# A fused retention and gated-MLP block on one core: w_out requested sooner, fewer filler matmuls, and the residual of batch 4 turned by DMA transposes

## The chip, the core and the metric

The kernel runs on one core of a Trainium2 chip. The core has five engines that run side by side: TensorE (PE, with its weight loads shown as PEld), VectorE (DVE), ScalarE (ACT), GpSimd (POOL) and SyncE (SP), which here only issues DMAs. Sixteen DMA engines serve all the queues. The metric is the device time of one execution in microseconds (us). Three runs of the kernel before gave 213.83, 214.52 and 214.94 us; their median is 214.52 us.

## The reference

Retention first (8 batches, 8 heads, 576 positions, head size 64), then a gMLP block over the heads put side by side (512 wide), with the retention's output `x` as the residual:

```
scores = q @ k.T / sqrt(64);  ret = scores * gamma_h ** (i - j) for i >= j, else 0
x = (ret @ v), heads side by side: [8, 576, 512]
h = gelu_tanh(x @ w_in);  u, v = halves of h (512 each)
v_n = (v - mean(v)) / sqrt(var(v) + 1e-6) * g_ln
v_s = w_sg @ v_n (over the 576 positions) + b_sg
out = x + (u * v_s) @ w_out
```

All inputs and the output are float32. The kernel multiplies in bfloat16 and adds up in float32.

## The kernel before, in words

The work is cut into 18 steps, `j = 0..17`. Steps 0 and 9 take the first 64 positions of four batches at once; each other step takes 256 positions of one batch, so that steps 10 and 11 are the two halves of batch 4, and 12 to 17 those of batches 5, 6 and 7. Output rows come in tiles of 128: pair `p` of batches has nine of them, `m = 0..8`; tile 4 (`MID`) holds the first 64 positions of both batches.

One step goes through these stages. q, k and v arrive by DMA from SP. POOL scales q and k to bfloat16 (`qb`, `kb`) and casts v (`vb`), ACT and DVE doing some of them at the start. q and k are transposed: q by DMA transposes on SP from step 5 on (`turn`, L288), k on PE (`T`, L271), except for the last steps, where k too is turned by DMA. Then `quarters` (L451) makes on PE the scores `sc` of the next step, its state products `zp` and the outputs `ot` of this one; `intra` (L469) copies `ot` to `xT`, the retention's output, *transposed* (features on partitions). `V` and `U` multiply `xT` by the two halves of w_in. When a batch has both halves, `release` queues its units: `W` (the product over positions with w_sg, L600, and the product with u on DVE, L602) and `O` (the product with w_out, L622). The loop at L804 takes units from that list by the numbers in `slots`. The order on each engine is written out by hand: an engine runs its instructions in the order in which the program lists them, and SP and POOL issue DMAs in that order too.

The residual of an `O` unit is added in one of two ways. For batches 0 to 4, `xT` is turned back on PE: four matmuls of 128x128 with `xT` as weights and the identity as data (L626) add it to the product in PSUM, and ACT copies the tile to `ob` (L628). For batches 5 to 7 a DMA transpose on SP (`turn_x`, L297, issued at L304) has put the residual into `xn`, with rows on partitions; PE then does only the four matmuls of L622, and DVE adds `xn` while it empties PSUM (L630). The first tiles of the pairs (`m == MID`) use the first way, but for the last pair. A DMA of SP then stores the tile (L635).

Three other places bear on the change. At the start, `spin(16)` (L672) runs 48 matmuls on zeros of 171, 171 and 170 columns while the first data arrive. The weights w_out are fetched by a DMA that POOL issues, since it casts to bfloat16 (`load_w(SB)`, L187). And step 3's state product ends in `cast_zb` on POOL (L391), which waits for a DVE addition (L390).

Of the kernel before, what the change touches and what calls it, by code (L numbers as in the profile page):

```python
# [12 lines left out]
BF = mybir.dt.bfloat16  # L13
# [6 lines left out]
def kernel(  # L20
# [193 lines left out]
    idle = psD.tile([128, 512], F32, name="idle", tag="d")  # L214
    SPIN = 171, 171, 170

    def spin(n):
        for _ in range(n):
            for c in SPIN:
                nc.tensor.matmul(idle[:, :c], fill[:, :128], fill[:, :c], start=True, stop=True)  # L220


# [15 lines left out]
    def xT(p, m):  # L238

        b = 2 * p + (m > MID)  # L240
        if m == MID:
            if (p, m) not in xTs:
                xTs[p, m] = xup.tile([128, KK, 128], BF, name="xm")
            return xTs[p, m]
        if b not in xTs:
            xTs[b] = xup.tile([128, MID, KK, 128], BF, name="xT")
        return xTs[b][:, m % (MID + 1)]
# [49 lines left out]
    def turn_x(j):  # L297

        p, m = chunk(j, 0)
        if j % 2 == NB % 2:  # L300
            xns[j // 2] = ld.tile([128, MID, KK, 128], BF, name="xn", tag="vf")
        b, i = place(j)[1], 2 * place(j)[2]
        x = xns[j // 2][:, i:i + 2]
        nc.sync.dma_start_transpose(x.rearrange("p c k t -> p (c k) t"),  # L304
                                    xTs[b][:, i:i + 2].rearrange("p c k t -> p (c k t)"))
        for c in range(2):
            xns[p, m + c] = x[:, c].rearrange("p k t -> p (k t)")
# [251 lines left out]
    def U(j, n):  # L559

        p, m = chunk(j, n)
        hu = psD.tile([128, KK, 128], F32, name="hu", tag="d")
        if m == MID:
            uTs[p, MID] = u = xup.tile([128, KK, 128], BF, name="um")
            for c in range(KK):
                for kk in range(KK):
                    nc.tensor.matmul(hu[:, c, :], w_in[:, kk, 128 * c:128 * c + 128], xT(p, m)[:, kk],  # L567
                                     start=(kk == 0), stop=(kk == KK - 1), skip_group_check=True)
            nc.scalar.activation(u, hu[:], Act.Gelu_apprx_tanh)
        else:  # L570
            b, i = place(j)[1], 2 * place(j)[2]
            xT(*chunk(j, 0))
            at, f = 64 * (b % 2) + 128 * i, KK // 2 * n
            for c in range(KK // 2):
                o = hu[:, 2 * c:2 * c + 2, :]
                for kk in range(KK):
                    nc.tensor.matmul(o, w_in[:, kk, 128 * (f + c):128 * (f + c) + 128], xTs[b][:, i:i + 2, kk, :],  # L577
                                     start=(kk == 0), stop=(kk == KK - 1), skip_group_check=True)
            nc.scalar.activation(uT(b)[:, f:f + KK // 2, at:at + 256],  # L579
                                 hu[:].rearrange("p (c i) t -> p c (i t)", i=2), Act.Gelu_apprx_tanh)  # L580
        tick()
# [23 lines left out]
    def O(p, m):  # L605
        unit[0] = "O"
        r = slice(128 * m, 128 * m + 128)
        xn = xns.get((p, m))
        b, s0 = 2 * p + (m > MID), LEAD + 128 * (m % (MID + 1))
        if xn is None or m == MID:  # L610
            ob = w3.tile([128, DM], F32, name="ob", bufs=6)
        else:
            if b not in obs:
                obs[b] = ld.tile([128, MID, DM], F32, name="obs", tag="qk")
            ob = obs[b][:, m % (MID + 1)]

        n = 2 if (b, m) == (B - 1, NT - 1) else 1
        for h in range(n):
            op = psD.tile([128, DM // n], F32, name="op", tag="d")
            f = slice(DM // n * h, DM // n * (h + 1))  # L620
            for c in range(KK):
                nc.tensor.matmul(op[:], gTs[p][:, c, r], w_out[:, c, f], start=(c == 0),  # L622
                                 stop=(xn is not None and c == KK - 1), skip_group_check=True)
            if xn is None:
                for kk in range(KK):
                    nc.tensor.matmul(op[:, 128 * kk:128 * kk + 128], xT(p, m)[:, kk], ident[:],  # L626
                                     start=False, stop=True, skip_group_check=True)
                nc.scalar.copy(ob[:, f], op[:])  # L628
            else:
                nc.vector.tensor_tensor(ob[:, f], op[:], xn[:, f], op=Alu.add)  # L630
            if m == MID:
                for e in range(2):
                    nc.sync.dma_start(out[2 * p + e, :LEAD, :], ob[64 * e:64 * e + 64])
            else:
                (nc.scalar if h else nc.sync).dma_start(out[b, s0:s0 + 128, f], ob[:, f])  # L635
        tick()
# [32 lines left out]


    HEAD = 3
    spin(16)  # L672
    build_masks()
    clear_wL()
    fill_consts()
# [104 lines left out]
    cast(4, "q", nc.gpsimd)  # L780
    cast(4, "v", nc.scalar)
    load(6)
    Sc(3, 0)
    Z(3, 0)
    load_w(SB)
    run(1)
    Sc(3, 1)
    T(4, "k")
# [15 lines left out]
    for j in range(HEAD, NB):  # L804
        nx = j + 1 < NB
        slots = where[share.get(j, 6)] if nx else (3, 0, 1, 1)

        more = lambda x, p: load(x, (p,)) if HEAD + 3 < x < NB else None
        if j + 2 < NB:
            turn(j + 2, "q")  # L810
            if j + 5 >= NB or j in EXTRA:
                turn(j + 2, "k")
        more(j + 3, k)
        more(j + 3, v)

        if nx:
            quarters(j)
        else:
            inter(j)
            run(1)  # L820
            intra(j)
        if j + 3 < NB:
            f = lambda j=j: cast(j + 3, "q", nc.gpsimd)
            if j in (4,5):
                after_pow[j] = f
            else:
                later(4, f)
        run(slots[0] if nx else slots[0] - 1, "O" if place(j)[2] == 0 and j > 4 else "W")
        more(j + 4, q)
        V(j, 0, (3, 5) if j == HEAD else (2, 5))  # L830
        if not nx:
            V(j, 1)
        for x in {NB - 4: (NB - 6,), NB - 3: (NB - 5, NB - 4), NB - 2: (NB - 3, NB - 2), NB - 1: (NB - 1,)}.get(j, ()):
            turn_x(x)
        if j == NB - 3:
            turn_mid(B // 2 - 1)
        run(slots[1], "O")
        if nx:
            V(j, 1)
        if j + 5 < NB and j not in EXTRA:  # L840
            T(j + 2, "k")
        U(j, 0)
        if nx:
            run(slots[2], "O")
        if j + 3 < NB:
            cast(j + 3, "k", nc.gpsimd)
            cast(j + 3, "v", nc.gpsimd)
        U(j, 1)
        if nx and place(j)[1] is not None and place(j)[2] == (place(j)[1] + 1 == GB) and place(j)[1] + 1 < B:
            start_state(place(j)[1] + 1)  # L850
        run(slots[3] - 1, "W")
        held.append(j)
        run(1, "W")
        held.clear()
        release(j)
# [36 lines left out]
```

## Time and profile before

| what | value |
|---|---|
| runs | 213.83, 214.52, 214.94 us; median 214.52 us |
| profiled execution | 214.26 us, of which the span from the first to the last instruction is 212.5 us |
| granted TensorE clock, mean | 0.996 |
| PE busy | 200.2 us, 94% of the span |
| DVE / ACT / POOL busy | 165.7 us / 127.1 us / 130.0 us |
| queue q1 (SP's and ACT's DMAs) | 45.10 MB in 85440 packets, packet time 92.6% of sixteen engines' span |

A row of the timeline gives the start in us, the length in us, engine, line, operation, output and inputs, and how many instructions were merged; in brackets stands the idle time ahead of it and what ended that. A row of the chain of waits gives the start, the length, and the work that the end of the program goes back to. A row of instructions by line ends in "busy, mean ns of one, idle before". A window's row gives, for a stretch of time, each engine's busy time with the number of instructions, then the granted clock, the DMA share (packet time over sixteen engines' time; it can exceed 1, since packets overlap) and the rate in GB/s. Among the DMA issues, the last number is the time from issue to landing. SPq is SP's queue of instructions.

### The profile page before, as it was taken

What the parts mean: (1) busy time and instruction counts of PE and PEld (TensorE: products, weight loads), DVE (VectorE), ACT (ScalarE), POOL (GpSimd) and SP (SyncE); (2) the same over time, 40 slices, a digit from 0 to 9 for tenths busy, and PEclk for the clock granted to TensorE, in tenths of its full rate; (3) what the DMA queues carried; (4) which work ended last, traced back from release to release, by engine and by line L of the source; (5) the groups of instructions that cost most, each with busy time, mean ns of one, the idle gap of its engine ahead of it and who ended that gap; (6) DMA issues with size and microseconds to landing.
All of it is one profiled execution on the core that took longest, in us unless ns stands there. A gap on an engine that the chain in (4) does not pass through costs nothing.

```text
span 212.5 us, 7628 instructions
## 1 busy us (share of the span) xinstructions
PE 200.2 (94%) x3238; PEld 143.9 (68%) x3238; DVE 165.7 (78%) x345; ACT 127.1 (60%) x221; POOL 130.0 (61%) x143
## 2 busy tenths in 40 slices
PE   7698989999699999999999999999999999999990
PEld 7665667676567687668767776768776876666650
DVE  7766888889878899667876897668956997958771
ACT  4364677674577876786777657776648465565000
POOL 8065998989666779848475999675775712111000
PEclk9999999999999999999999999999999999999998
DMA  6999999999999998999989999769999999632435
GB/s 158 251 316 286 318 252 278 251 290 225 189 221 303 204 224 170 261 191 334 222 205 269 269 269 227 224 166 329 145 300 191 296 194 154 167 84 52 148 97 201
DMA packets 88178, 47.44 MB, mean 223 GB/s; under 512 B 26000, under 2 KB 82640, under 8 KB 88144
## 3 DMA queue, kind: packets, MB, share of 16 engines
q1 hardware_dynamic: 85440, 45.10, 92.6%
q0 software_dynamic: 1472, 1.20, 3.5%
q10 hardware_dynamic: 1232, 0.66, 1.2%
q8 instruction: 25, 0.41, 0.8%
q14 instruction: 9, 0.07, 0.1%
HBM read 32.79 MB, written 9.44 MB: 199 GB/s over the span
## 4 chain that ended last, share of the span: by engine, by line
PE 70%; DMA 4%; DVE 3%; POOL 1%; ACT 0%; issue 0%; DVEq 0%; POOLq 0%
PE wp L600 18%; PE op L622 15%; PE hv L493 11%; PE hu L577 10%; DMA qT<-qb 4%; PE sc L343 4%; PE ot L477 4%; PE ot L435 3%; PE tp L277 3%; PE op L626 2%; PE hu L567 1%; PE zp L368 1%; DVE rs L511 1%; DVE bst L506 1%; PE zf L368 1%; POOL rs L502 1%
## 5 line engine op out<-in xcount | busy, mean ns | idle before, releaser
L347 DVE TENSOR_TENSOR ret<-sc,mask 128x512 bf16<-128x512 f32 x72 | 45.9, 682 | 12.1 <-PE zp L368 7.1
L502 POOL TENSOR_TENSOR rs<-rs,mhalf 128x2 f32<-128x2 f32 (+1 forms) x21 | 21.1, 1006 | 41.8 <-DVE rs L511 41.2
L600 PE MATMUL wp<-wT,vn 128*128 128x288 bf16 x256 | 41.7, 286 | 0.4 <-DVE wT L250 0.3
L622 PE MATMUL op<-w_out,gT 128*128 128x512 bf16 (+1 forms) x148 | 36.1, 374 | 0.0
L602 DVE TENSOR_TENSOR gT<-wp,uT 128x288 bf16<-128x288 f32 x64 | 27.8, 451 | 9.7 <-PE wp L600 8.8
L577 PE MATMUL hu<-xT,w_in 128*128 128x256 bf16 x256 | 32.7, 273 | 0.0
L493 PE MATMUL hv<-w_in,xT 128*128 128x512 bf16 x128 | 32.1, 379 | 0.2
L268 POOL TENSOR_TENSOR kb<-qk,gk 128x1024 bf16<-128x1024 f32 x16 | 30.9, 1928 | 1.1 <-DMA qk<-in_k_dram 1.1
L506 DVE BATCH_NORM_STATS2 bst<-vg 128x6 f32<-128x512 f32 x36 | 24.7, 686 | 7.8 <-ACT vg L496 7.8
L268 POOL TENSOR_TENSOR qb<-qk,gq 128x1024 bf16<-128x1024 f32 x15 | 29.4, 1963 | 1.9 <-DMA qk<-in_q_dram 1.9
L520 DVE SCALAR_TENSOR_TENSOR vc<-vg,mv,g_bc 128x512 f32<-128x512 f32 x36 | 29.5, 819 | 0.5
L250 ACT CAST xT<-ot 128x512 bf16<-128x512 f32 x30 | 20.2, 739 | 16.2 <-PE ot L477 16.2
L600 PEld LDWEIGHTS <-vn 128*128 128x128 bf16 x256 | 24.4, 98 | 7.9 <-ACT vn L535 0.6
L496 ACT ACTIVATE vg<-hv 128x512 f32<-128x512 f32 x36 | 21.5, 597 | 13.3 <-PE hv L493 13.0
L577 PEld LDWEIGHTS <-w_in 128*128 128x128 bf16 x256 | 24.4, 98 | 4.2
L535 ACT ACTIVATE vn<-vc,rs 128x512 bf16<-128x512 f32 x32 | 22.5, 723 | 5.3 <-POOL rs L502 5.0
L579 ACT ACTIVATE uT<-hu 128x512 bf16<-128x512 f32 x32 | 19.0, 601 | 9.4 <-PE hu L577 9.3
L622 PEld LDWEIGHTS <-gT 128*128 128x128 bf16 x148 | 13.6, 98 | 11.3
L493 PEld LDWEIGHTS <-xT 128*128 128x128 bf16 x128 | 11.9, 98 | 10.6 <-ACT xT L250 0.7
L250 ACT COPY kT<-tp 128x1024 bf16<-128x1024 bf16 x15 | 15.1, 1009 | 5.9 <-PE tp L277 5.8
L600 PE MATMUL wp<-wL,vnm 128*128 128x288 bf16 x64 | 18.3, 287 | 0.0
L343 PE MATMUL sc<-qT,kT 64*64 64x128 bf16 x576 | 15.4, 219 | 2.4 <-DMA qT<-qb 1.7
(115 smaller groups left out, 303.0 us busy)
## 6 DMA issues: line engine op xcount, KB each, us to landing
qk<-in_k_dram SPq DMA_DIRECT2D x16, 512.0 KB, 5.4
qk<-in_q_dram SPq DMA_DIRECT2D x16, 512.0 KB, 7.5
vf<-in_v_dram SPq DMA_DIRECT2D x16, 512.0 KB, 7.4
out_dram<-ob SPq DMA_DIRECT2D x20, 256.0 KB, 5.5
out_dram<-obs SPq DMA_DIRECT2D x11, 256.0 KB, 2.4
wst<-in_moe_w_in_dram SPq DMA_DIRECT2D x2, 1024.0 KB, 7.7
vf<-in_v_dram SPq DMA_DIRECT2D x8, 128.0 KB, 4.1
out_dram<-ob SPq DMA_DIRECT2D x8, 128.0 KB, 2.7
```

What stands on the lines that cost most here:

```text
L250: (eng.copy if eng is nc.scalar else eng.tensor_copy)(o, i)
L268: eng.tensor_tensor(o, src, tab[:, kind].rearrange("p a h -> p h a").unsqueeze(3).to_broadcast([128, H, 2, D]), op=Alu.mult)
L343: nc.tensor.matmul(sc[r][cc, x, a, :], kT[rr, a, kk, cc], qT[rr, :, kk, cc], start=True, stop=True, skip_group_check=True)
L347: nc.vector.tensor_tensor(s["ret"][:, r, 2 * g:2 * g + 2], sc[r][:], mask[1 if place(j)[1] is None else 0][:].unsqueeze(1).to_broadcast([1 ...
L493: nc.tensor.matmul(hv[:], xT(p, m)[:, kk], w_in[:, kk, F2:], start=(kk == 0), stop=(kk == KK - 1))
L502: nc.gpsimd.tensor_tensor(st["rs"][:], st["rs"][:], mhalf[:, :n], op=Alu.pow)
L506: nc.vector.bn_stats(bst[:], vg[:])
L520: nc.vector.scalar_tensor_tensor(vc[:], vg[:], st["mv"][:, k, 0:1], g_bc[:], op0=Alu.subtract, op1=Alu.mult)
L577: nc.tensor.matmul(o, w_in[:, kk, 128 * (f + c):128 * (f + c) + 128], xTs[b][:, i:i + 2, kk, :], start=(kk == 0), stop=(kk == KK - 1), ski ...
L600: nc.tensor.matmul(ps[:], vns[p, m][e][:, 128 * c:128 * c + 128], w, start=(x == 0), stop=(x == SB - 1))
L602: nc.vector.tensor_tensor(gTs[p][:, c, col:col + HS], ps[:], uTs[b][:, c, half * HS:half * HS + HS], op=Alu.mult)
L622: nc.tensor.matmul(op[:], gTs[p][:, c, r], w_out[:, c, f], start=(c == 0), stop=(xn is not None and c == KK - 1), skip_group_check=True)
```

## The change

Four things are changed. `spin(16)` becomes three matmuls of 512 columns and 13 rounds of the old three, the same number of columns in 42 matmuls in place of 48. `load_w(SB)` is called ahead of `Sc(3, 0)` and `Z(3, 0)`. At step 12 both halves of batch 4 (steps 10 and 11) are turned by DMA transposes, into a tile of their own; the `O` units of batch 4 so take the second way, and still write to `ob`. Two buffers get fewer copies to make room for that tile: `xm` three in place of four, `um` two in place of four.

```
-    spin(16)
+    spin(3, (512,))
+    spin(13)
...
     load(6)
+    load_w(SB)
     Sc(3, 0)
     Z(3, 0)
-    load_w(SB)
...
-                xTs[p, m] = xup.tile([128, KK, 128], BF, name="xm")
+                xTs[p, m] = xup.tile([128, KK, 128], BF, name="xm", bufs=3)
...
-            xns[j // 2] = ld.tile([128, MID, KK, 128], BF, name="xn", tag="vf")
+            xns[j // 2] = (xup.tile([128, MID, KK, 128], BF, name="xn", bufs=1) if j < NB - 6 else
+                           ld.tile([128, MID, KK, 128], BF, name="xn", tag="vf"))
...
-            uTs[p, MID] = u = xup.tile([128, KK, 128], BF, name="um")
+            uTs[p, MID] = u = xup.tile([128, KK, 128], BF, name="um", bufs=2)
...
-        if xn is None or m == MID:
+        if xn is None or m == MID or b < B - 3:
             ob = w3.tile([128, DM], F32, name="ob", bufs=6)
...
-        for x in {NB - 4: (NB - 6,), NB - 3: (NB - 5, NB - 4), NB - 2: (NB - 3, NB - 2), NB - 1: (NB - 1,)}.get(j, ()):
+        for x in {NB - 6: (NB - 8, NB - 7), NB - 4: (NB - 6,), NB - 3: (NB - 5, NB - 4), NB - 2: (NB - 3, NB - 2), NB - 1: (NB - 1,)}.get(j, ()):
             turn_x(x)
```

The added lines move the numbers of what follows by one or two: L304, L391, L602, L622 and L630 become L305, L392, L603, L623 and L631.

SP's queue at step 12 and the start of step 13, before (q, k, v are the loads of later steps, `ob` the stores of tiles, the first `qT` here is step 14's, the second step 15's):

```order
L292 DMA_TRANSPOSE qT<-qb 128x8x128
L88 DMA qk<-in_k_dram 128x8x128
L88 DMA vf<-in_v_dram 128x8x128
L635 DMA out_dram<-ob 128x512 x2
L88 DMA qk<-in_q_dram 128x8x128
L292 DMA_TRANSPOSE qT<-qb 128x8x128
L292 DMA_TRANSPOSE kT<-kb 128x8x128
L88 DMA qk<-in_k_dram 128x8x128
L88 DMA vf<-in_v_dram 128x8x128
```

and after:

```order
L292 DMA_TRANSPOSE qT<-qb 128x8x128
L88 DMA qk<-in_k_dram 128x8x128
L88 DMA vf<-in_v_dram 128x8x128
L636 DMA out_dram<-ob 128x512 x2
L88 DMA qk<-in_q_dram 128x8x128
L305 DMA_TRANSPOSE xn<-xT 128x8x128 x2
L292 DMA_TRANSPOSE qT<-qb 128x8x128
L292 DMA_TRANSPOSE kT<-kb 128x8x128
L88 DMA qk<-in_k_dram 128x8x128
L88 DMA vf<-in_v_dram 128x8x128
```

Two transposes now stand ahead of step 15's `qT` and `kT` and of all that SP issues after them.

DVE's queue where batch 4's four `O` units are worked off, before (`ret` are the masked scores, `gT` the product of a W unit, `bst` the statistics of V):

```order
L602 TENSOR_TENSOR gT<-wp,uT 128x288
L347 TENSOR_TENSOR ret<-sc,mask_158 128x512
L390 TENSOR_TENSOR kept<-zp,kept 128x256
L347 TENSOR_TENSOR ret<-sc,mask_158 128x512 x2
L390 TENSOR_TENSOR kept<-zp,kept 128x256
L347 TENSOR_TENSOR ret<-sc,mask_158 128x512
L602 TENSOR_TENSOR gT<-wp,uT 128x288
L506 BN_STATS bst<-vg 128x6
```

and after:

```order
L603 TENSOR_TENSOR gT<-wp,uT 128x288
L631 TENSOR_TENSOR ob<-op,xn 128x512 x2
L348 TENSOR_TENSOR ret<-sc,mask_158 128x512
L391 TENSOR_TENSOR kept<-zp,kept 128x256
L348 TENSOR_TENSOR ret<-sc,mask_158 128x512 x2
L391 TENSOR_TENSOR kept<-zp,kept 128x256
L348 TENSOR_TENSOR ret<-sc,mask_158 128x512
L631 TENSOR_TENSOR ob<-op,xn 128x512 x2
L603 TENSOR_TENSOR gT<-wp,uT 128x288
L507 BN_STATS bst<-vg 128x6
```

Four additions have come to DVE, two ahead of the scores of step 15 and two behind them; ACT's four copies to `ob` at this place are gone, and PE's sixteen matmuls of L626.

POOL's queue at the request for w_out, before (`zb` is the state that step 3's second half reads; the last `qb`, `kb` and `vb` are step 5's):

```order
L268 TENSOR_TENSOR kb<-qk,gk 128x8x2x64
L268 TENSOR_TENSOR qb<-qk,gq 128x8x2x64
L391 CAST zb<-state_777 128x256
L187 DMA w_out<-in_moe_w_out_dram 128x4x512
L268 TENSOR_TENSOR qb<-qk,gq 128x8x2x64
L268 TENSOR_TENSOR kb<-qk,gk 128x8x2x64
L250 CAST vb<-vf 128x8x2x64
```

and after:

```order
L268 TENSOR_TENSOR kb<-qk,gk 128x8x2x64
L268 TENSOR_TENSOR qb<-qk,gq 128x8x2x64
L187 DMA w_out<-in_moe_w_out_dram 128x4x512
L392 CAST zb<-state_771 128x256
L268 TENSOR_TENSOR qb<-qk,gq 128x8x2x64
L268 TENSOR_TENSOR kb<-qk,gk 128x8x2x64
L250 CAST vb<-vf 128x8x2x64
```

The request and the cast have changed places.

More of the change, by code (lines that the diff above doesn't have):

```diff
@@ L215, with spin @@
     SPIN = 171, 171, 170
-    def spin(n):
+    def spin(n, cols=SPIN):
         for _ in range(n):
-            for c in SPIN:
+            for c in cols:
                 nc.tensor.matmul(idle[:, :c], fill[:, :128], fill[:, :c], start=True, stop=True)
```

## The prediction

> **What bounds the kernel now.** I read the page's busy times first, then PE's waits, then the chain of waits, and then the queues at the two places that the change touches.
>
> The page, the first row of PE's waits from 40 us on (the longest in total; the others there come to 0.5 us), and a window over the steady part:
>
> ```profile
> span 212.5 us, 7628 instructions
> PE 200.2 (94%) x3238; PEld 143.9 (68%) x3238; DVE 165.7 (78%) x345; ACT 127.1 (60%) x221; POOL 130.0 (61%) x143
> ...
> PE sc L343 <- DMA qT<-qb: 1.7, 1, 1.7
> ...
> 60.00:207.00 147.00, 146.73 (x2268) 103.42 (x2267) 115.82 (x239) 92.85 (x164) 84.65 (x82) 1.00 0.94 211
> ```
>
> From 60 to 207 us PE is busy for 146.73 of 147.00 us at a granted clock of 1.00. After 40 us it waits for another engine or a DMA once for long: 1.7 us for `qT`, a DMA transpose. So work taken off PE in the steady part is time saved, unless something then arrives late; and that one wait is the other thing to be won.
>
> The chain of waits at that wait, and where batch 4's `O` units run:
>
> ```profile
> 49.65 8.63 DMA qT<-qb
> 58.32 0.63 PE sc L343 x30
> ...
> 156.12 0.22 PE op L626 x4
> 156.35 0.86 PE op L622 x4
> 157.21 0.22 PE op L626 x4
> 157.43 0.45 PE ot L435 x12
> ...
> 160.11 0.22 PE op L626 x4
> ...
> 161.20 0.22 PE op L626 x4
> 161.42 0.65 PE hv L493 x3
> ```
>
> The reader is to see that the units stand on the chain without a gap (156.12 + 0.22 is 156.34, where the next product begins), each with 0.22 us for turning the residual.
>
> **The change, part by part.**
>
> *PE loses sixteen matmuls.* Four groups of 0.22 us: 4 x 0.22 = 0.88 us, all on the chain. The range of this term is 0.8 to 0.9, since rows round; nothing hides it, as PE is full ahead of and behind it.
>
> *DVE takes what ACT did.* The rows are DVE's timeline and the groups by line:
>
> ```profile
> 158.26 0.69 DVE L347 TENSOR_TENSOR ret<-sc,mask 128x512 bf16<-128x512 f32 x1 [2.08 <-PE zp L368]
> 160.73 0.68 DVE L347 TENSOR_TENSOR ret<-sc,mask 128x512 bf16<-128x512 f32 x1
> 162.94 0.46 DVE L602 TENSOR_TENSOR gT<-wp,uT 128x288 bf16<-128x288 f32 x1 [1.53 <-PE wp L600]
> ...
> L628 ACT COPY ob<-op 128x512 f32<-128x512 f32 x23 | 13.5, 586 | 3.9 <-PE op L626 3.9
> L630 DVE TENSOR_TENSOR obs<-op,xn 128x512 f32<-128x512 f32 x11 | 7.5, 688 | 2.7 <-PE op L622 2.6
> ```
>
> Two additions of 0.69 us (1.4 together) fall into the idle 2.08 us ahead of the scores at 158.26, and two into the idle 1.53 us ahead of 162.94. The second pair can begin only at 161.4, when the last `ret` ends, and the `gT` behind them then comes some 0.3 us late against a PE that is 0.88 us ahead. PE does not read that `gT` until a later `O`. I take 0; the ends are 0 and 0.3 lost. ACT gains 4 x 0.59 = 2.3 us, of which nothing is on the chain.
>
> *Two transposes on SP's queue.* SP's timeline around the new place, its later `kT`, the landing times (of all three `kT`, and of the last, step 17's), PE's first scores of steps 15 and 16, and the rate of a stretch in which transposes run alone:
>
> ```profile
> 143.47 0.43 SPq L88 DMA_DIRECT2D qk<-in_q_dram  x1
> 144.01 5.13 SPq L292 DMA_TRANSPOSE qT<-qb  x1
> 149.29 1.39 SPq L292 DMA_TRANSPOSE kT<-kb  x1
> 160.05 1.78 SPq L292 DMA_TRANSPOSE kT<-kb  x1
> 165.00 2.65 SPq L304 DMA_TRANSPOSE xn<-xT  x1
> 169.95 1.97 SPq L292 DMA_TRANSPOSE kT<-kb  x1
> ...
> kT<-kb SPq DMA_TRANSPOSE x3, 4.8
> ...
> kT<-kb SPq DMA_TRANSPOSE x1, 4.7
> ...
> 157.67 0.24 PE L343 MATMUL sc<-qT,kT 64*64 64x128 bf16 x1
> ...
> 167.59 0.24 PE L343 MATMUL sc<-qT,kT 64*64 64x128 bf16 x2
> ...
> 174.00:176.00 2.00, 2.00 (x18) 1.41 (x17) 1.93 (x5) 0.83 (x2) 0.87 (x1) 1.00 1.19 257
> ```
>
> The queue is backed up at 144 us: `qT`'s issue takes 5.13 us where `kT`'s takes 1.39. The new transposes are queued right here, behind the load at 143.47, and their data (`xT` of steps 10 and 11) are long there. So the first takes over the 5.13 us, until 149.2, and the second and `qT` take about 1.4 each; `kT` is issued at 152.0 and not at 149.29, when POOL's `kb` frees it. Landing 4.8 us later it is there at 156.8. PE asks for it at 157.67, or 157.2 once two of the four units are shorter by 0.44 together. So 0.4 us are left of 3.6.
>
> The loads behind (`k`, `v` and `q` of later steps) go out 2.7 us later, and POOL's casts of them wait up to 1.5 us; POOL has room there, idle 82 of 212 us. Step 16 has a smaller margin: `kT` lands at 160.05 + 4.8 = 164.85, PE asks at 167.59, or 166.7 with 0.88 us saved: 1.9 us. Each transpose is 128 x 1024 x 2 bytes = 262 KB; at the 257 GB/s of the last row it costs 1.0 us of the engines, two 2.0. Were all of that still in the queue at 160, PE would wait 0.1 us. What makes me take 0: ahead of step 17's `kT` (169.95) the kernel already sends one `xn` (165.00), and that `kT` (4.7 us) lands as fast as the median of the three (4.8). Some of what is pushed in is worked off before the next `kT`. The ends for two transposes are 1.0 (half of it absorbed) and 5.4, twice the 2.7 between the two `xn` of these rows, the slowest pair here:
>
> ```profile
> 171.97 2.67 SPq L304 DMA_TRANSPOSE xn<-xT  x2
> ...
> xn<-xT SPq DMA_TRANSPOSE x1, 3.5
> ...
> xn<-xT SPq DMA_TRANSPOSE x1, 4.9
> ```
>
> (issued at 171.97 and some 1.35 later, landed at 175.5 and 178.2). At 5.4 PE would wait 5.4 - 1.9 = 3.5 us.
>
> [...]
>
> *w_out requested sooner.* POOL, SP, the landings and the window from 49 to 58 us:
>
> ```profile
> 43.52 1.92 POOL L268 TENSOR_TENSOR qb<-qk,gq 128x1024 bf16<-128x1024 f32 x1
> 46.46 0.40 POOL L391 CAST zb<-state 128x256 bf16<-128x256 f32 x1 [1.02 <-DVE state L390]
> 46.80 0.86 POOL L187 DMA_DIRECT2D w_out<-in_moe_w_out_dram  x1
> 47.68 1.94 POOL L268 TENSOR_TENSOR qb<-qk,gq 128x1024 bf16<-128x1024 f32 x1
> ...
> vf<-in_v_dram SPq DMA_DIRECT2D x1, 512.0 KB, 10.6
> w_out<-in_moe_w_out_dram POOLq DMA_DIRECT2D x1, 512.0 KB, 9.6
> ...
> 49.00:58.00 9.00, 7.48 (x168) 5.46 (x163) 8.19 (x16) 5.24 (x11) 7.28 (x8) 1.00 1.19 196
> ```
>
> The issue of 0.86 us moves into the 1.02 us for which POOL stands idle ahead of `zb`, from 45.44 to 46.30; `zb` stays at 46.46. The `qb` behind it starts at about 46.85, 0.83 us sooner, and with it the request for the transpose that PE waits for. That is the upper end, 0.83 us, and up to 1.7 if w_out, away 1.36 us earlier, also frees the DMA engines for it. The lower end is nothing: the `v` load ahead of that transpose was issued at 46.72 and took 10.6 us, to 57.3, and the transpose, although requested at 49.65, landed only at 58.28. It was behind the load, not behind POOL, in a stretch with a DMA share of 1.19. I take 0.25, near the lower end, because the row of the `v` load is the nearest; a loss is possible too (w_out goes ahead of the loads on which POOL waits), some 0.3.
>
> [...]
>
> *The fillers.* They end before anything needs PE:
>
> ```profile
> 8.74 0.62 PE L277 MATMUL tp<-ident,klead 128*128 128x128 bf16 x8 [1.60 <-DVE klead L268]
> ```
>
> The columns stay the same (16 x 512 in 48 matmuls, then in 42), and PE idles 1.60 us for `klead` behind them: 0, between 0.1 lost and 0.1 won, as long as that wait remains. The two smaller pools (`xm`, `um`) add no wait on the engines' queues: 0.
>
> *Sum.* 0.88 + 0.25 = 1.13 us off. The profiled execution took 214.26 us, 1.8 around its span of 212.5, and lies 0.26 below the median of 214.52; against the median this gives 213.4 us, 0.5% less. About 0.5%, or 1.07 us, is what the runs can tell from no change: they lie 1.1 us apart.
>
> **The rivals.**
>
> 1. *w_out moves nothing.* The transpose of 49.65 lands at 58.3 as before, PE waits its 1.7 us, and only the 0.88 is won: 213.6. For it speaks the DMA share of 1.19 and the `v` load; against it that POOL requests the transpose 0.83 us sooner.
>
> 2. *Step 16's `kT` is late.* The two transposes stay in the queue from 144 on, where the share is above 1, and `kT` lands behind PE's need at 166.7. From 1.9 us of delay on PE waits; from 2.8 the gain of 0.88 is gone; from 3.9 the kernel is slower by more than 0.5%. At the upper end of 5.4 PE waits 3.5 us: 214.52 - 0.88 - 0.25 + 3.5 = 216.9. For it: the 5.13 us that an issue takes at 144, the 2.7 between two `xn`. Against: one `xn` ahead of `kT` costs that `kT` nothing today.
>
> 3. *w_out clears the way.* With w_out's bytes gone earlier, PE's wait of 1.7 us vanishes: 214.52 - 0.88 - 1.7 = 211.9. Against it stands the `v` load.
>
> **How the numbers follow.** The forecast, 212.8 to 213.5 (0.88 and between 0.15 and 0.83 from w_out, no late `kT`): 0.42. Rival 1, 213.5 to 213.9: 0.22. Rival 2: 0.30, of which 0.17 beyond 215.6 and 0.13 between 213.6 and 215.6. Rival 3: 0.06. Faster by over 0.5% (below 213.45): 0.42 and 0.06, 0.48. Within: 0.22 and 0.13, 0.35. Slower: 0.17. The range from 212.2 to 216.0 leaves out most of rival 3 and the worst tenth of rival 2; the forecast's own range is 212.8 to 213.5.
>
> **What the profile of the changed kernel would show.** Right: in the chain, the units of batch 4 follow each other at 0.86 us with no L626 between; the four additions on DVE start by 157.3 and by 162; PE's waits name no `kT`, and from 60 to 207 us PE stays busy to within 0.3 us. For w_out: issue at 45.4, landing near 55, and `qT`'s landing at 57.4 to 58.2, the wait below 1.7 us. Wrong: a wait of PE for `kT` or `qT` near 157, 167 or 177 us, with landings more than 7 us behind the issue; DVE's `gT` at 162.9 holding an `O` back; or a wait of 1.7 us that has grown, because w_out's bytes now pass the `q` load that POOL casts next.

## The result, and the profile after

The changed kernel takes 214.18 us (median of 22 runs, 212.71 to 216.82); the kernel before, run beside it, takes 214.15 us (22 runs, 212.43 to 218.77). The ratio is 0.9998, with a 95% interval from 0.9974 to 1.0023: no difference. (Medians are of all runs; the ratios, here and below, leave out the slow runs, which lie over 1.5% above the fastest of their kernel.) The forecast was 213.4 us. The time lies in the wide range of 212.2 to 216.0, but outside the forecast's own 212.8 to 213.5, in the band that the prediction gave to its second rival (213.6 to 215.6, chance 0.13). The 0.88 us that sixteen matmuls should have won do not show in the total, and the question is where they went.

The profiled execution of the changed kernel took 213.85 us. Its page, its row of the DMA queue q8 ("instruction"), its window from 60 to 207 us, and its list of PE's waits from 40 us on:

```profile
span 212.1 us, 7586 instructions
...
PE 199.6 (94%) x3216; PEld 142.4 (67%) x3216; DVE 169.0 (80%) x349; ACT 125.2 (59%) x217; POOL 130.0 (61%) x143
...
q8 instruction: 25, 0.41, 0.9%
...
60.00:207.00 147.00, 144.51 (x2242) 101.81 (x2241) 118.41 (x239) 88.86 (x157) 84.07 (x81) 1.00 0.99 212
...
PE ot L478 <- issue: 1.5, 1, 1.5
PE sc L344 <- DMA kT<-kb: 0.9, 2, 0.7
PE wp L601 <- DVE wT L250: 0.4, 2, 0.2
```

Four readings follow. PE is 0.6 us less busy in all, at the same granted clock of 1.00 in the steady part, and DVE and ACT have traded work as foreseen (DVE 3.3 us more, ACT 1.9 us less). The steady part, which was full before (146.73 of 147.00), is not full any more: 2.49 us of it are empty. The 1.7 us for which PE waited for `qT` near 56 us are gone from the list. In their place stand 1.5 us of "issue" and 0.9 us for `kT`, the very wait of which the second rival spoke.

To see where time is won and lost, the steps of PE are used as a clock. The first `ot` of a step (L435, L436 after the change) marks its start. The rows of steps 10, 11, 12 and 17, first of the kernel before (a second profiled execution of it, of which more below), then of the changed kernel:

```profile
116.29 0.52 PE L435 MATMUL ot<-qT,zb 64*64 64x128 bf16 x12
...
126.53 0.52 PE L435 MATMUL ot<-qT,zb 64*64 64x128 bf16 x12
...
136.17 0.52 PE L435 MATMUL ot<-qT,zb 64*64 64x128 bf16 x12
...
185.76 0.63 PE L435 MATMUL ot<-qT,zb 64*64 64x128 bf16 x16
```

```profile
115.28 0.52 PE L436 MATMUL ot<-qT,zb 64*64 64x128 bf16 x12
...
126.47 0.52 PE L436 MATMUL ot<-qT,zb 64*64 64x128 bf16 x12
...
136.23 0.52 PE L436 MATMUL ot<-qT,zb 64*64 64x128 bf16 x12
...
186.46 0.63 PE L436 MATMUL ot<-qT,zb 64*64 64x128 bf16 x16
```

The changed kernel comes to step 10 at 115.28, 1.0 us ahead; by step 11 all but 0.06 us of that is gone, and it comes to step 12 at 136.23, no longer ahead: from step 10 to step 12 it takes 20.95 us where the kernel before takes 19.88. That is before the first of the new transposes is issued, and before any unit of batch 4 runs. Read from the same rows of all profiles (differences of their starts, in us; "to 5" is from the span's start to step 5, "rest" from step 17 to the span's end):

| kernel | to 5 | 5 to 10 | 10 to 12 | 12 to 17 | rest | span |
|---|---|---|---|---|---|---|
| before | 66.87 | 50.35 | 19.87 | 49.59 | 25.79 | 212.5 |
| before_again | 65.91 | 50.38 | 19.87 | 49.59 | 25.74 | 211.5 |
| wout | 66.55 | 50.36 | 19.92 | 49.59 | 25.77 | 212.2 |
| before_order | 64.46 | 50.36 | 19.60 | 49.61 | 25.74 | 209.8 |
| spare2 | 66.64 | 51.13 | 19.96 | 49.59 | 25.70 | 213.0 |
| spare4 | 65.37 | 51.13 | 20.97 | 54.26 | 25.39 | 217.1 |
| residual | 64.80 | 50.36 | 20.95 | 48.88 | 25.62 | 210.6 |
| after | 64.91 | 50.36 | 20.95 | 50.23 | 25.61 | 212.1 |
| after_again | 65.23 | 51.13 | 20.97 | 48.69 | 25.65 | 211.7 |
| early | 65.49 | 50.37 | 20.96 | 49.96 | 26.18 | 213.0 |
| gap | 65.21 | 50.36 | 20.96 | 48.70 | 26.13 | 211.4 |
| gap_again | 65.18 | 50.37 | 20.96 | 48.70 | 25.61 | 210.8 |
| gap_order | 65.21 | 51.26 | 20.17 | 49.17 | 26.09 | 211.9 |

The names are those of the experiments below. The head ("to 5") scatters by 2.4 us from one execution to the next. The three stretches from step 5 to 17 mostly take one of a few values each, which repeat within 0.1 us, while the totals of single runs lie some 4 us apart. So the stretches tell what the totals cannot, though one kernel can take different values in two executions (`after` and `after_again`). The changed kernel saves 0.89 us from step 12 to 17 (48.70 for 49.59) where nothing comes late, loses 1.08 us from step 10 to 12, and in one of its two profiles loses 1.53 us more from step 12 to 17.

### The profile page after: what moved, and what is told of

Read it like the earlier page. It is cut to its first block, busy times and chain, and to the rows that moved or that the text cites. A ratio compares the mean times of both kernels' runs of the same rounds, so it can differ in the third digit from the quotient of the medians.

```text
span 212.1 us, 7586 instructions
## 1 busy us (share of the span) xinstructions
PE 199.6 (94%) x3216; PEld 142.4 (67%) x3216; DVE 169.0 (80%) x349; ACT 125.2 (59%) x217; POOL 130.0 (61%) x143
## 4 chain that ended last, share of the span: by engine, by line
PE 58%; DMA 11%; POOL 3%; SPq 3%; issue 2%; ACT 2%; DVE 1%; DVEq 0%; POOLq 0%
PE wp L601 14%; PE op L623 11%; PE hv L494 9%; PE hu L578 8%; DMA qk<-in_q_dram 7%; PE sc L344 3%; PE ot L478 3%; PE tp L277 3%; PE ot L436 2%; DMA qk<-in_k_dram 2%; SPq L292 2%; PE op L627 2%; DMA kT<-kb 2%; POOL qb L268 1%; PE hu L568 1%
## 5 line engine op out<-in xcount | busy, mean ns | idle before, releaser
L623 PE MATMUL op<-w_out,gT 128*128 128x512 bf16 (+1 forms) x148 | 35.7, 374 | 0.0
L603 DVE TENSOR_TENSOR gT<-wp,uT 128x288 bf16<-128x288 f32 x64 | 27.8, 450 | 9.3 <-PE wp L601 8.5
L521 DVE SCALAR_TENSOR_TENSOR vc<-vg,mv,g_bc 128x512 f32<-128x512 f32 x36 | 30.1, 837 | 0.5
L623 PEld LDWEIGHTS <-gT 128*128 128x128 bf16 x148 | 13.7, 98 | 11.8
L250 POOL CAST vb<-vf 128x1024 bf16<-128x1024 f32 x14 | 15.1, 1076 | 2.8 <-DMA vf<-in_v_dram 2.8
```

The lines of the kernel that those rows point to most:

```text
L250: (eng.copy if eng is nc.scalar else eng.tensor_copy)(o, i)
L521: nc.vector.scalar_tensor_tensor(vc[:], vg[:], st["mv"][:, k, 0:1], g_bc[:], op0=Alu.subtract, op1=Alu.mult)
L603: nc.vector.tensor_tensor(gTs[p][:, c, col:col + HS], ps[:], uTs[b][:, c, half * HS:half * HS + HS], op=Alu.mult)
```

## The experiments

**One part of the change alone.** `wout` is the kernel before with only this edit:

```
     load(6)
+    load_w(SB)
     Sc(3, 0)
     Z(3, 0)
-    load_w(SB)
```

> The kernel before with the request for w_out moved ahead of step 3's scores and state, and nothing else. Theory (the request matters): PE's wait of 1.7 us for the transpose of step 5's q near 57 us shrinks to under 0.5 us, POOL issues w_out at 45.3 to 45.5 us and not 46.8, the transpose lands near 56 us, and the time falls by 1 to 1.9 us (ratio 0.991 to 0.995). Rival (the bytes only change places; what moved that landing in the changed kernel was how far the loads of the first 45 us had come): the time stays within 0.3% (ratio 0.997 to 1.003), and the landing follows the loads ahead of it: early if step 6's v load is issued near 45 us, late if near 46.7 us.

It took 213.89 us (12 runs), ratio 0.999 (0.9957 to 1.0023); the theory's 0.991 to 0.995 lie outside. In its profile PE does not wait for `qT`, but not because w_out went out sooner in time: POOL issues it at 46.57 us, the `v` load goes out at 46.52, and the transpose lands at 57.3. PE itself comes late, to step 4 at 57.56 us (55.98 in the first profile of the kernel before). `residual` is the other large part alone, that is, all lines of the change on `xm`, `um`, `xn`, `ob` and `turn_x`, without the fillers and without the move of w_out:

```
-        if xn is None or m == MID:
+        if xn is None or m == MID or b < B - 3:
...
+        for x in {NB - 6: (NB - 8, NB - 7), NB - 4: (NB - 6,), ...
```

> The kernel before with batch 4's residual turned by DMA transposes, and neither the move of w_out nor the change of the fillers. Theory (the sixteen matmuls are saved and then waited away): PE is 0.88 us ahead at 165 us, waits 0.5 to 1.5 us for step 16's or 17's kT near 167 and 177 us, and the time stays within 0.3% (ratio 0.997 to 1.002). Rival (the transposes cost nothing and the gain was lost to chance elsewhere, such as the 1.5 us that PE stood still near 117 us): no wait for kT above 0.2 us, ratio 0.994 to 0.997.

It took 213.84 us, ratio 1.000 (0.9959 to 1.004). In its profile step 16's `kT` lands at 166.0 us, and only 0.18 us of the 0.89 are lost behind step 12 (48.88 for 48.70): less than the theory's 0.5 to 1.5 us. The 0.25 us of w_out's term (0.1%) are too little for such intervals to show, and the 0.88 us of the residual's (0.4%) lie at the edge of theirs, so more had to be learnt from the stretches.

**The kernel before, once more.** `before_again` is the kernel before without any edit.

> The kernel before once more, for a second profile of it. If PE's wait of 1.7 us for the transpose of step 5's q is the program's own, it is there again, 1.2 to 2.0 us. If it hangs on how far the loads of the first 45 us have come, it differs by a microsecond or more from the first profile, and the issue of step 6's v load (46.7 us there) with it. Ratio 0.998 to 1.002.

It took 214.62 us, ratio 1.0023 (0.9985 to 1.0062). Its list of PE's waits from 40 us on:

```profile
PE ot L477 <- issue: 0.6, 1, 0.6
PE hu L577 <- issue: 0.4, 1, 0.4
```

The 1.7 us for `qT`, which headed this list in the profile that the prediction read, are not there. Of the eleven other traces of the table only one has any of it (0.8 us in `spare2`, below, where w_out is fetched late as before). Two things differ. One is how far the loads had come: the `v` load ahead of that transpose was issued at 46.72 us in the first profile and took 10.6 us; in `before_again` it was issued at 45.20 us and took 7.5, and the transpose landed at 56.6 and not at 58.3. The other is PE, which came to step 4 at 56.92 and not at 55.98. The wait comes and goes from one execution of the same kernel to the next.

**Where the transposes stand in the queue.** In `early` the two new transposes are issued at the start of step 12, behind step 14's `qT` (at 140.44 us), and no longer near its end:

```
             turn(j + 2, "q")
+            if j == NB - 6:
+                turn_x(NB - 8)
+                turn_x(NB - 7)
...
-        for x in {NB - 6: (NB - 8, NB - 7), NB - 4: ...
+        for x in {NB - 4: ...
```

> The changed kernel with its two new transposes issued one place sooner: at the start of step 12, behind step 14's q transpose and ahead of the loads for step 15, near 139 us, where the DMA share is 0.6 and not 1.2. All else is the changed kernel's. Theory (the transposes are late for kT because they are queued behind a backlog): step 16's and 17's kT land in time, PE's waits near 167 and 177 us fall under 0.3 us in all, and the time is 0.5 to 1.2 us below the changed kernel's, ratio to before 0.993 to 0.998. Rival (the queue is full from 139 to 178 us as a whole, so that the same bytes cost the same wherever they are put): PE waits 0.8 to 1.5 us again, ratio 0.998 to 1.002.

214.62 us, ratio 1.003 (0.9994 to 1.0065), and 49.96 us from step 12 to 17: `kT` still comes late, PE waits 1.1 us for it. Three us earlier is not enough: step 16's `kT` is issued at 161.54 and lands at 167.8, no sooner than in the changed kernel (161.02 and 166.8). In `gap` they are issued one step earlier still, with one character changed:

```
-        for x in {NB - 6: (NB - 8, NB - 7), ...
+        for x in {NB - 7: (NB - 8, NB - 7), ...
```

> The changed kernel with its two new transposes issued at step 11, behind the load of step 15's q near 132.6 us, so that they run in the stretch from 135 to 139 us in which the queue of the second profile of before is nearly empty. Measured by the stage from ACT's copy done of step 11 to that of step 17, which takes 58.92 us in both profiles of before. Theory (the transposes delay kT by the 2 us that they take from a queue which is full from 139 to 178 us): PE waits for no kT above 0.3 us, the stage takes 58.0 to 58.3 us, and the time falls by 0.3 to 0.9 us (ratio 0.995 to 0.999). Rival (the delay comes from elsewhere, such as a lagging DMA engine): a wait of 0.5 us or more for kT, stage 58.7 to 59.6 us.

SP's timeline shows it, first of the changed kernel, then of `gap`:

```profile
143.39 6.79 SPq L305 DMA_TRANSPOSE xn<-xT  x2
150.29 1.98 SPq L292 DMA_TRANSPOSE qT<-qb  x1
152.38 1.25 SPq L292 DMA_TRANSPOSE kT<-kb  x1
...
161.02 3.71 SPq L292 DMA_TRANSPOSE kT<-kb  x1
```

```profile
132.99 3.64 SPq L305 DMA_TRANSPOSE xn<-xT  x2
...
149.01 1.47 SPq L292 DMA_TRANSPOSE kT<-kb  x1
...
159.30 2.25 SPq L292 DMA_TRANSPOSE kT<-kb  x1
```

The two new transposes take SP 3.64 us at 133 us, and 6.79 us at 143 us, where the queue takes them more slowly. In `gap` step 15's `kT` goes out at 149.01, as before the change (149.29), and step 16's at 159.30 (160.05 before). It lands at 164.6, where the changed kernel's lands at 166.8. `gap` takes 48.70 us from step 12 to 17 and waits for no `kT`: here the sixteen matmuls are won in full. It took 213.4 us, ratio 0.9966 (0.9926 to 1.0006). The same kernel once more:

> gap once more. If its gain is of the kernel and not of the session: ratio 0.994 to 0.999 again, the stage from step 11 to step 17 at 58.0 us, kT of step 16 landing by 165, and the two steps from 10 to 12 at 20.96 us. If not: a ratio of 1.000 or more, or one of these marks missing.

213.57 us, ratio 0.9959 (0.9918 to 1.0001), again 48.70 us there, step 16's `kT` landing at 165.1, and 20.96 us from step 10 to 12. Both intervals still include 1, if barely; the stretch does not depend on them. From step 5 to step 17 `gap` is 0.2 us longer than the kernel before (120.02 for 119.81), since it loses 1.09 us from step 10 to 12. So if the 0.4% are a gain at all, they lie in the head, where one execution differs from the next by more.

**Transposes and nothing else.** `spare2` is the kernel before with two transposes of batch 4's `xT` at the change's place whose result nobody reads (and with the smaller pools); `spare4` has four of them. The residual of batch 4 is added on PE, as before.

```
+        if j == NB - 6:
+            spare = xup.tile([128, MID, KK, 128], BF, name="spare", bufs=1)
+            for x in range(2):
+                nc.sync.dma_start_transpose(spare[...], xTs[4][...])
```

> The kernel before, residual on PE as it was, with two DMA transposes of xT into a tile that nothing reads, at the place of the change's two; the buffers xm and um as in the change. Theory (each takes 1.0 us of a full queue): kT of steps 15 and 16 land about 2 us later than in before; PE's margin of 2.7 us covers it; the stage from step 11 to step 17 takes 58.9 to 59.2 us. Rival (part of it is worked off before step 16's kT): kT of step 16 lands less than 1 us later.

> The same with four such transposes. Theory: kT of step 16 lands 4 us later, PE's margin of 2.7 us is gone, PE waits 1.2 to 2.5 us for kT, the stage takes 60.1 to 61.4 us, and the time rises by 1.2 to 2.5 us (ratio 1.005 to 1.012). Rival (worked off): no wait, stage 58.9 to 59.2 us, ratio 0.998 to 1.002.

`spare2` ran once, 214.8 us, and its stretch from 12 to 17 is 49.59 us, as without them. Step 16's `kT` lands at 167.0 us in it, 2.2 us later than in the first profile of the kernel before (164.85), while PE comes to that step only 0.6 us later: the delay is the theory's, not the rival's. `spare4` took 219.01 us (4 runs), ratio 1.0226 (1.0161 to 1.0291), with 54.26 us there. First row of its PE waits:

```profile
PE sc L343 <- DMA kT<-kb: 4.0, 3, 2.3
```

That is about twice what was expected of four. SP takes 11.73 us to issue them at 144.18 us, and step 15's `kT` goes out at 157.38, 8.1 us later than before the change (149.29): 2 us for each transpose, where the prediction counted 1.0 from a stretch in which transposes ran alone. So the cost sets in between two and four transposes for a PE as slow as before, and at two for a PE that is 0.88 us faster, in those executions in which `kT` lands behind its need. That is a margin of about two transposes, as the prediction had it, and no smooth slope: the first two are free, the next two cost 4.67 us.

**The changed kernel once more.**

> The changed kernel once more, for a second profile. Theory (0.88 us saved, and the queue 2 to 3 us late against a margin of 1.9 us): kT of step 16 lands 0 to 1.3 us behind PE's need, the stage from step 11 to step 17 takes 58.0 to 59.6 us (59.56 in the first profile). The wait for step 5's q near 57 us is under 0.3 us, as in the second profile of before. Rival (the first profile's waits for kT were an accident): stage 58.0 to 58.1 us, no wait for kT.

213.82 us, ratio 0.999 (0.995 to 1.0031). Here 48.69 us pass from step 12 to 17, without a wait for `kT`, though step 16's `kT` lands at 166.8 us, as in the first profile. PE simply comes later: it had lost 0.77 us between steps 5 and 10, and has the first scores of it at 166.92, 0.31 us behind the step's first `ot` (166.61), as always when nothing is waited for. In the first profile that first `ot` starts at 165.52, so the scores could have begun at 165.83. The two places where the first profile's PE waits for it:

```profile
166.81 0.71 PE L344 MATMUL sc<-qT,kT 64*64 64x128 bf16 x32 [0.65 <-DMA kT<-kb]
...
177.18 0.24 PE L344 MATMUL sc<-qT,kT 64*64 64x128 bf16 x2 [0.29 <-DMA kT<-kb]
```

The stretch is lengthened by 1.53 us and not only by these 0.94: the list counts a wait only from where PE has nothing left, and in the time ahead of it PE ran, alone, the `ot` that it else slips between the scores (166.81 - 165.83 is 0.98 us for step 16 by itself). Whatever PE wins ahead of step 16 it gives back there, as long as the queue delivers at 166.8; in `residual`, where `kT` lands at 166.0 and the first `ot` starts at 165.40, it gives back 0.18 us.

**The stretch from step 10 to step 12.** It takes either 19.9 or 20.96 us, and the rows of DVE and POOL tell the two kinds apart. Of `before_again`, DVE, then POOL:

```profile
123.05 0.75 DVE L520 SCALAR_TENSOR_TENSOR vc<-vg,mv,g_bc 128x512 f32<-128x512 f32 x1
...
124.66 0.96 DVE L511 TENSOR_SCALAR rs<-mv 128x2 f32<-128x2 f32 x1
...
123.20 2.39 POOL L268 TENSOR_TENSOR qb<-qk,gq 128x1024 bf16<-128x1024 f32 x1
125.77 1.08 POOL L502 TENSOR_TENSOR rs<-rs,mhalf 128x2 f32<-128x2 f32 x1 [0.17 <-DVE rs L511]
```

And of the changed kernel:

```profile
122.99 1.67 DVE L521 SCALAR_TENSOR_TENSOR vc<-vg,mv,g_bc 128x512 f32<-128x512 f32 x1
...
122.18 1.93 POOL L268 TENSOR_TENSOR qb<-qk,gq 128x1024 bf16<-128x1024 f32 x1
125.83 1.08 POOL L503 TENSOR_TENSOR rs<-rs,mhalf 128x2 f32<-128x2 f32 x1 [1.72 <-DVE rs L512]
```

In the first, `vc` starts 0.15 us ahead of POOL's `qb`. It takes its usual 0.75 us, and it is `qb` that is stretched, from 1.93 to 2.39 us. In the second `qb` is first, and `vc` takes 1.67 us, ending at 124.66, 0.55 us behind the end of `qb`, a little less than its usual 0.75. DVE's statistics of the second tile, POOL's power (`rs`) and ACT's `vn` follow from there. So in these rows the one that comes first takes its usual time and the other is lengthened, `qb` by 0.46 us in the first and `vc` by 0.92 in the second; `vc` starts 0.15 us ahead in the one and 0.81 us behind in the other, and the stretch takes 19.87 us in the one and 20.95 in the other. Why the two hold each other up, no trace shows; the "port" of the two expectations below was their author's guess.

What makes `vc` late is PE's "issue" wait inside step 10. Of `before_again` and of the changed kernel, PE's rows at it:

```profile
117.45 0.52 PE L477 MATMUL ot<-ret,vb 64*64 64x128 bf16 x23
118.59 0.30 PE L477 MATMUL ot<-ret,vb 64*64 64x128 bf16 x7 [0.63 <-issue]
```

```profile
116.43 0.63 PE L478 MATMUL ot<-ret,vb 64*64 64x128 bf16 x29
118.59 0.24 PE L478 MATMUL ot<-ret,vb 64*64 64x128 bf16 x1 [1.53 <-issue]
```

From the last start ahead of the wait to the next, PE stands 0.85 us in the one and 1.75 in the other. Over the traces of the table (but for the two `order` kernels, below) it is 0.27 to 0.93 us in the four where `vc` comes ahead of `qb`, and 0.98 to 1.77 us in the seven where it comes behind: the turn flips between `spare2` (0.93) and `spare4` (0.98). With `gap_order` this was put to the test. It is `gap` with POOL's cast of `qb` in step 10 put behind the power, so that `vc` cannot meet it; `before_order` is the kernel before with the same edit:

```
-            if j in (4,5):
+            if j in (4, 5, NB - 8):
                 after_pow[j] = f
```

> The changed kernel with the two transposes at step 11, and POOL's qb cast of step 10 put behind its rs (the power that the last vn of step 10 needs). From PE's first ot of step 10 to that of step 12 the kernels so far took either 19.9 us (before, before_again, wout, spare2) or 20.96 us (residual, after, after_again, early, gap, spare4), 1.07 more, and in all of the second kind DVE's vc at about 123 us starts after POOL's qb has begun, lasts 1.7 to 2.5 us and ends 0.55 us after qb does; in the first kind it starts ahead of qb and lasts 0.75 to 0.96 us. Theory (the turn at the port): whenever PE's wait in step 10 is above about 1.0 us, vc comes behind qb and the step's normalisation comes 1.07 us late. Then with qb behind rs vc lasts 0.75 us in any case, and the two steps take what PE needs, 9.4 + 9.64 + its wait in step 10 (1.2 in gap): 20.2 to 20.4 us, 0.6 to 0.8 less than gap; against before about 0.994. Rival: the 1.07 us are PE's own waiting (its instructions come late), and the length of vc only shows it: 20.9 to 21.0 us as in gap, and a ratio like gap's, 0.997.

> The kernel before with POOL's qb cast of step 10 put behind its rs, and nothing else. Theory (the turn at the port): before holds the turn already (vc ahead of qb), so that PE's need, 9.4 + 9.64 + its wait in step 10 (0.3 to 1.0), stands: 19.3 to 20.0 us for the two steps, ratio 0.997 to 1.001. Rival (qb later makes qT of step 13 and the loads behind it late): over 20.0 us there or a wait for qT at step 12, ratio above 1.002.

In `gap_order` the stretch falls from 20.96 to 20.17 us, although PE's wait is as long as in `gap` (1.13 against 1.21 us). DVE and POOL:

```profile
123.56 0.75 DVE L521 SCALAR_TENSOR_TENSOR vc<-vg,mv,g_bc 128x512 f32<-128x512 f32 x1
...
125.49 1.07 POOL L503 TENSOR_TENSOR rs<-rs,mhalf 128x2 f32<-128x2 f32 x1 [2.07 <-DVE rs L512]
126.53 1.93 POOL L268 TENSOR_TENSOR qb<-qk,gq 128x1024 bf16<-128x1024 f32 x1
```

So in `gap` 0.8 us of the loss was the turn of `vc` and `qb`, and the rest is PE's own wait. In the changed kernel itself the shares are the other way round. Step 10 takes 9.4 us and PE's wait in all thirteen traces (11.19 us in the changed kernel, 10.23 in `before_again`), and step 11, 9.6 us where nothing is late, takes 9.76 in the changed kernel, 10.32 in `gap` and 10.60 in `spare4`. (In the first profile of the kernel before, which has the shortest wait, it takes 10.21: there DVE's `rs` runs beside `qb` and takes 1.33 us in place of 0.17.) The longer wait thus costs the changed kernel 0.96 us by itself, and the late `vc` only 0.12 more, since PE comes late as well; with `qb` moved it would take an estimated 20.8 us for the two steps (9.4 + 1.75 + 9.6), 0.15 less than it does. The total did not follow: 214.86 us, ratio 1.0029 (0.9994 to 1.0065). In the profile 0.90 us went between steps 5 and 10, where PE stood 0.94 us for "issue" near 67 us (among the other traces only `spare2`, `spare4` and `after_again` lose time between these steps, 0.77 us each). Another 0.47 us went from step 12 to 17: a `rs` of DVE that took 0.96 us at 154.54 delayed the two new additions that stand ahead of the masking of the scores, so that PE waited 0.4 us until 157.77, and step 16's `kT` landed at 166.8 again. Whether these belong to this kernel or to the execution, one profile does not tell; the total gives no sign that the edit helps beside the others. `before_order` took 213.47 us, ratio 0.9979 (0.994 to 1.0017), with 19.60 us in the stretch, as expected of a kernel that mostly had the turn already.

**The fillers alone.** The last part of the change, on the kernel before:

```
-    spin(16)
+    spin(3, (512,))
+    spin(13)
```

> The kernel before with the fillers of the change alone: 42 matmuls of the same columns. As forecast, 0: PE still waits for klead behind them (1.60 us before), ratio 1.000 within 0.003. Rival (twelve instructions less, six matmuls with their weight loads, move PE's later waits for its own instructions): the wait in step 10 is above 1.2 us, and the two steps there take 20.96 us in place of 19.9, +1.07 us, ratio 1.005.

214.82 us (10 runs), ratio 1.0031 (0.9998 to 1.0064): no gain, but the interval takes in the forecast's 1.000 as well as the rival's 1.005. Its profiled execution ran at a granted clock of 0.563 and a span of 335.0 us, an outlier among its own runs (the next is 216.27 us), so its trace cannot say whether the wait in step 10 changes with the fillers alone. The longer wait does not need them: `residual`, with the old fillers, has 1.46 us.

## Why the prediction was right and wrong

*PE loses sixteen matmuls: right.* 0.88 us were forecast, and 0.89 us are missing from the stretch of steps 12 to 17 in `gap`, `gap_again` and `after_again`.

*DVE takes what ACT did: right.* The four additions and the `gT` behind them, in DVE's timeline of the changed kernel:

```profile
155.30 0.69 DVE L631 TENSOR_TENSOR ob<-op,xn 128x512 f32<-128x512 f32 x1
156.16 0.69 DVE L631 TENSOR_TENSOR ob<-op,xn 128x512 f32<-128x512 f32 x1 [0.17 <-PE op L623]
156.95 0.69 DVE L348 TENSOR_TENSOR ret<-sc,mask 128x512 bf16<-128x512 f32 x1
...
160.02 1.27 DVE L631 TENSOR_TENSOR ob<-op,xn 128x512 f32<-128x512 f32 x2
161.21 0.44 DVE L603 TENSOR_TENSOR gT<-wp,uT 128x288 bf16<-128x288 f32 x1
```

The first two are done ahead of the scores, the second two ahead of `gT`, and PE waits for neither. Only in `gap_order` did PE wait for the first two (0.4 us, above): their room is not sure in every execution.

*Two transposes: the first `kT` right, the second wrong.* Step 15's was to be issued at 152.0 and to land at 156.8, in time. It was issued at 152.38 and landed at 155.6. The step that failed is "Some of what is pushed in is worked off before the next `kT`", by which the 2.0 us of transfers were to leave step 16's margin of 1.9 us untouched. Nothing was worked off: step 16's `kT` landed at 166.8 against 164.85 forecast from before, later by the full 2 us. Against `before_again`, which comes to step 12 at the same time, it is 2.9 us (163.9). Step 17's landed at 177.1 (174.6 in the first profile of before, 173.6 in the second). POOL's timeline shows how the delay is handed on, first in `before_again`, then in the changed kernel:

```profile
155.41 1.93 POOL L268 TENSOR_TENSOR kb<-qk,gk 128x1024 bf16<-128x1024 f32 x1
...
166.27 1.93 POOL L268 TENSOR_TENSOR kb<-qk,gk 128x1024 bf16<-128x1024 f32 x1
```

```profile
158.46 1.94 POOL L268 TENSOR_TENSOR kb<-qk,gk 128x1024 bf16<-128x1024 f32 x1 [2.96 <-DMA qk<-in_k_dram]
...
169.89 1.94 POOL L268 TENSOR_TENSOR kb<-qk,gk 128x1024 bf16<-128x1024 f32 x1 [2.67 <-DMA qk<-in_k_dram]
```

The loads behind the transposes come late, POOL casts late, and so the next transposes are requested late: what the queue owes is passed from step to step (`kT` is 2.0 us late at step 16 and 2.5 at step 17), in a stretch, 143 to 178 us, whose DMA share is 1.16. That POOL "has room there" was true and no help, since it is the data that it lacks. The one `xn` ahead of step 17's `kT` was a poor witness: before the change it was in the queue already, and the `kT` behind it was timed with it. And PE could have used step 16's `kT` at 165.83, not at the forecast 166.7, since this execution came to step 12 0.86 us sooner (136.23, 137.09 in the first profile of before). So it lost 1.0 us there and 1.5 with step 17, where 0.1 stood in the text as the price of nothing being worked off: the second rival's mechanism, with a price between the 0 that was taken and the 3.5 of its upper end.

*w_out: wrong in what it was measured against.* The request went out where the prediction put it, in POOL's timeline of the changed kernel:

```profile
45.34 0.86 POOL L187 DMA_DIRECT2D w_out<-in_moe_w_out_dram  x1
46.41 0.39 POOL L392 CAST zb<-state 128x256 bf16<-128x256 f32 x1 [0.21 <-DVE state L391]
46.77 1.92 POOL L268 TENSOR_TENSOR qb<-qk,gq 128x1024 bf16<-128x1024 f32 x1
```

(45.4 and 46.85 were forecast), and w_out landed at 53.6. But the term of 0.25 us, and the first and third rivals with it, shared out a wait of 1.7 us that a second execution of the kernel before does not have. Alone, the move gives a ratio of 0.999, within 0.4%. The head to step 5 is 64.91 to 65.49 us in the six traces with the changed head (the move of w_out and the fillers), and 64.46 to 66.87 in the seven others: perhaps steadier; a gain is not shown.

*What the sum did not have.* From step 10 to 12 the changed kernel loses 1.08 us, ahead of all that the change adds at step 12. The prediction read PE's 146.73 of 147.00 us as a steady part without slack to lose, and held the order of DVE and POOL there for fixed. Most of the loss (0.96 us) is PE's wait in step 10; the turn of `vc` and `qb`, which hung on 0.15 us, adds the rest. That wait lasts 1.13 to 1.77 us in all seven traces that have the residual's part of the change, and 0.27 to 0.98 us in all six that don't. That it goes with this part is plain; why is not settled. Up to that place the part alters nothing on PE, and the two `spare` kernels, with the same smaller pools, stay at 0.93 and 0.98. No row of the profile that the prediction read shows this wait: there it is 0.27 us, the shortest of all.

In sum, by the first profiles of both: head -1.96, step 10 to 12 +1.08, step 12 to 17 -0.89 + 1.53, rest -0.18, together -0.4 us, of which the head is scatter. Without the head, the 0.89 us won and the 1.08 lost cancel to within 0.2 us (0.1%) where `kT` is in time, and the measured ratio agrees with that. So it is luck, and the width of the range, that put the time inside it: of the sum the 0.88 us was won, and losses that the sum put at nothing took it back.

## What to carry to other kernels

A margin read from one profile is spent only once: if PE is made faster by 0.9 us and a queue slower by 2.0, both come out of the same 2.7 us, and in a queue as full as this one nothing was worked off (2.0 us late at step 16, 2.5 at step 17). Put new transfers where the queue has room, here ten us earlier (from 136 to 140 us the DMA share is 0.47 in `before_again`, from 139 to 178 it is 1.16), and check that by the landing time of the last transfer behind them. Before a wait is counted as something to win, look for it in a second execution of the same kernel; and measure by stretches between fixed instructions, which here take a few values that repeat within 0.1 us where totals scatter by 4, and more than one execution of each kernel.

## What the runs showed of the hardware beyond that

PE stood still, for 0.27 to 1.77 us in the thirteen traces, at a place that the program does not name. In the changed kernel, with twelve instructions (six matmuls and their weight loads) less ahead of it, the "issue" wait of step 10 comes six matmuls later in the program: 7 `ot` of L477 stand behind it in `before_again`, 1 of L478 in the changed kernel (the rows above); `residual`, with the old fillers, has 7. In all thirteen traces the same number of matmuls, 2012, stands ahead of it (counted by their weight loads where records of matmuls are missing). It thus goes with a count of instructions, and not with a semaphore that a trace shows ("issue" in the lists of waits). In each of the thirteen traces a packet of 16 KB of queue q8 ("instruction" on the page: 25 packets, 0.41 MB) ends 1.3 to 1.6 us before PE goes on; it starts between 0.68 us before and 0.81 us behind the step's first `ot`, and the wait is longer by about as much as the packet is later (to within 0.2 us). That the packet holds the instructions that PE lacks is an inference. If it does, the fetch is hidden at most of the 25 places: 21 of the packets come after 40 us, and from there on the list of PE's waits of the changed kernel names "issue" once, at this place, where 0.3 to 1.8 us stay open in the thirteen traces. By the page, 25 packets for 3216 matmuls and as many weight loads are one for every 257 of these instructions, an estimate that takes all packets for PE's; whose they are, no run shows.
